# Re-pacing attention beside the feed-forward: denser head pairs in down stages, exps ahead of squares, an earlier third batch, two up tiles held back

## The chip, the cores and the metric

The kernel runs on one core of one Trainium2 chip. The metric is the device time of one execution in microseconds (us). The core has five engines that run side by side: TensorE (PE in the profile, with its weight loads as PEld), VectorE (DVE), ScalarE (ACT), GpSimd (POOL) and SyncE (SP, which here only issues transfers). Each runs its own instructions in the order of the program, and semaphores make one wait for another.

## The reference, cut to what matters

```python
# q: 8 batches x 16 heads x 384 x 64;  k, v: 8 x 4 x 384 x 64   (four q heads share one k/v head)
scores = 1/sqrt(64) * q @ k^T                # per head 384 x 384
attn   = exp(scores - max) / sum
x      = attn @ v                            # 3072 tokens x 1024
h      = max(x @ w_in, 0)                    # "up":   1024 -> 2048
out    = (h*h) @ w_out                       # "down": 2048 -> 1024, float32
```

## The kernel before

A generator yields the feed-forward of one batch after another in small pieces of TensorE work; a main loop walks over the head pairs (two heads at once, 8 pairs per batch) and, between the steps of a pair, takes as many pieces as a credit allows ("filler"). So ScalarE can compute exps while TensorE does feed-forward. A batch's attention output must be transposed by a DMA into `xT` before its feed-forward may begin.

TensorE works in two halves of 64 rows that run at the same time (in the traces a matmul of 64 rows and 384 columns lasts 323 ns, and a pair of them enters each 162 ns). `push` writes the pieces for the low half at once and puts those for the high half into a queue; two clocks of the program's own (`clock["lo"]`, `clock["hi"]`) decide where the high pieces are merged in. These clocks are a plan made while the program is built; nothing measures them on the chip.

```python
def catch_up(until):                       # merges the queued high-half pieces
    while behind:
        job = behind[0]
        begin = max(clock["hi"], job["ready"])
        if begin > until:
            return
        ns, fn = job["hi"].pop(0)
        ...
        if not job["hi"]:
            behind.pop(0)
            ...
            if job["done"]:
                job["done"]()
...
def row_scores(p, half):                   # half a head pair: three score matmuls, then one exp
    ...
    both([piece(i) for i in range(3)])     # always into the same three PSUM banks, sc 0..2
    R.add("scalar", lambda e: e.activation(expT[p % NEX][:, 3 * half:3 * half + 3, :], sc_ps[:, 0:3, 0:S], AF.Exp, scale=0.125), ...)
...
def row_up(b, c, r, then=None):            # one up tile: 16 half-row matmuls
    ...
    def done():
        R.add("vector", lambda e: e.tensor_scalar_max(hr[r][:, :], acc[:, 0:S], 0.0), ...)             # relu
        R.add("scalar", lambda e: e.activation(h2T[b % 2][:, c, :], hr[r][:, :], AF.Square), ...)
        if then:
            then()
...
LULL = 11000.0
PER_PAIR = {1: 2600.0, 2: 3650.0, 3: 3650.0, **{b: 4800.0 for b in range(4, B + 1)}}    # filler, ns per pair
...
for n in range(NPB, NP + 1):
    b, c = n // NPB, n % NPB
    per = PER_PAIR[b]
    ahead = (per - 600.0) / 2
    ...
    if n == 2 * NPB:                       # the lull: no head pairs for 11 us
        fill(ahead)
        row_attend(n - 1)
        fill(2600.0)
        prepare(2)                         # transposes of k and q of batch 2, by DMA
        prepare_v(2)
        fill(LULL - 2600.0)
        ready[0] = 1
    if n < NP:
        row_scores(n, 0)
    fill(ahead)
    if n > NPB and n != 2 * NPB:
        row_attend(n - 1, ...)
    if n < NP:
        row_scores(n, 1)
    if 2 * NPB < n < (B - 1) * NPB:
        ...                                # prepare(b + 1) at c == 4, prepare_v(b + 1) at c == 7
    fill(per - ahead)
    ready[0] = max(0, b - 1)               # which batch's feed-forward may start
```

The down stages of batches 2 to 7 work on pairs of batches and on sums of blocks (seven products instead of eight, as in Strassen's method). Those sums (`a_late`, on DVE) need the squares of the last up tiles, so the end of the up stage of a pair of batches is a chain: up tile, relu, square, sums, next product.

The softmax here doesn't subtract the row's maximum and nothing guards it: scores larger than these inputs give would overflow.

## Time and profile before

| | before |
|---|---|
| time, median | 435.67 us (435.36 to 437.12) |
| PE busy, PEld busy | 95%, 67% |
| granted TensorE clock | 1.0 |
| chain of waits | PE 85%, DVE 6%, ACT 6% |

From the page of the kernel before: busy times, the rows of TensorE and its clock in 40 slices, the chain that ended last, and the groups of exps and squares (count, then busy us and mean ns of one, then idle us before them and its releaser).

```profile
PE 410.9 (95%) x6061; PEld 292.2 (67%) x6061; DVE 203.1 (47%) x419; ACT 217.8 (50%) x284; POOL 48.4 (11%) x62
PE   8999888998999998999999998998999999998995
PEclk9999999999999999999999999999999999999999
PE 85%; DVE 6%; ACT 6%; DMA 2%; issue 1%; DVEq 0%
L474 ACT ACTIVATE expT<-sc_ps 128x1152 bf16<-128x1152 f32 x112 | 126.3, 1127 | 85.8 <-PE sc_ps L470 62.7
L529 ACT ACTIVATE h2T<-hr 128x384 bf16<-128x384 f32 x122 | 63.5, 521 | 68.4 <-DVE hr L527 66.8
```

PE is the bound, but 95% overstates how full it is: with only one of the two row halves at work it counts as busy. The Trainium skill ("Perfetto Trace Analysis", section "Identifying the Most-Contended Engine") says that matmul busy time misjudges the distance to the limit and names weight-load busy time (beside the share of peak work) instead. This trace agrees for the whole: PEld is busy 67%, and by stage it goes up and down where PE hardly does. From the windows of the kernel before (start:end, length, then busy us and count per engine, granted clock, DMA share and GB/s):

```profile
36.00:76.00 40.00, 34.66 (x570) 24.05 (x570) 11.92 (x26) 22.73 (x27) 4.22 (x4) 1.00 1.12 162
146.00:176.00 30.00, 27.22 (x490) 21.86 (x486) 15.22 (x31) 19.37 (x27) 0.83 (x1) 1.00 0.61 105
256.00:306.00 50.00, 46.60 (x772) 37.03 (x769) 23.21 (x50) 30.57 (x43) 4.96 (x5) 1.00 0.54 65
366.00:396.00 30.00, 27.81 (x321) 16.00 (x319) 13.46 (x27) 10.46 (x20) 0.00 (x0) 1.00 0.02 4
```

Between 36 and 76 us PE is busy for 34.66 of 40 us and PEld for 24.05: here the prediction's count of matmuls finds the most lost, 9.8 us. The waits view (engine, line and tile that waited, whom it waited for: us in total, times, longest) says on what:

```profile
ACT h2T L529 <- DVE hr L527: 66.8, 80, 2.2
PE sc_ps L470 <- ACT expT L474: 6.0, 11, 0.7
PE f_ps L638 <- DVE a_late L580: 3.1, 3, 1.3
PE f_ps L521 <- DMA xT<-o_sb: 1.9, 2, 1.3
PE sc_ps L521 <- DMA xT<-o_sb: 1.7, 1, 1.7
```

And the timeline of one head pair in that stage (start, length, engine, line, tiles; in brackets the idle time before and who ended it):

```profile
46.88 0.56 DVE L527 TENSOR_SCALAR hr<-f_ps 128x384 f32<-128x384 f32 x1 [0.65 <-PE po L484]
47.48 0.52 ACT L529 ACTIVATE h2T<-hr 128x384 bf16<-128x384 f32 x1 [1.31 <-DVE hr L527]
47.91 1.11 ACT L474 ACTIVATE expT<-sc_ps 128x1152 bf16<-128x1152 f32 x1
...
49.07 0.50 PE L470 MATMUL sc_ps<-qT,kT 64*128 64x384 bf16 x3 [0.58 <-ACT expT L474]
```

The scores for the exp at 47.91 were issued at 46.81, but ACT first waits for the relu, does the square, and only then the exp; the next scores, which need the same PSUM banks, start at 49.07 after an idle PE.

### The profile page before, as it was taken

What the parts mean: (1) busy time and instruction counts of PE and PEld (TensorE: products, weight loads), DVE (VectorE), ACT (ScalarE), POOL (GpSimd) and SP (SyncE); (2) the same over time, 40 slices, a digit from 0 to 9 for tenths busy, and PEclk for the clock granted to TensorE, in tenths of its full rate; (3) what the DMA queues carried; (4) which work ended last, traced back from release to release, by engine and by line L of the source; (5) the groups of instructions that cost most, each with busy time, mean ns of one, the idle gap of its engine ahead of it and who ended that gap; (6) DMA issues with size and microseconds to landing.
All of it is one profiled execution on the core that took longest, in us unless ns stands there. A gap on an engine that the chain in (4) does not pass through costs nothing.

```text
span 433.3 us, 13205 instructions
## 1 busy us (share of the span) xinstructions
PE 410.9 (95%) x6061; PEld 292.2 (67%) x6061; DVE 203.1 (47%) x419; ACT 217.8 (50%) x284; POOL 48.4 (11%) x62
## 2 busy tenths in 40 slices
PE   8999888998999998999999998998999999998995
PEld 4665665686877777886666787876766787554552
DVE  2664332276522554465564344454654445455442
ACT  4865663066654666565443576665444464332010
POOL 5831010003002100210003000220000000000000
PEclk9999999999999999999999999999999999999999
DMA  8999995739913981195228930296223210000222
GB/s 231 196 197 204 205 183 68 161 108 105 154 52 78 190 138 25 24 129 116 93 70 143 199 98 20 31 129 110 73 74 98 92 44 22 2 2 0 98 98 97
DMA packets 96103, 45.02 MB, mean 104 GB/s; under 512 B 74416, under 2 KB 90032, under 8 KB 96048
## 3 DMA queue, kind: packets, MB, share of 16 engines
q0 software_dynamic: 34288, 16.65, 31.3%
q1 hardware_dynamic: 58720, 25.28, 26.4%
q10 hardware_dynamic: 3040, 2.26, 1.7%
q8 instruction: 47, 0.77, 0.8%
q14 instruction: 8, 0.07, 0.1%
HBM read 35.65 MB, written 12.58 MB: 111 GB/s over the span
## 4 chain that ended last, share of the span: by engine, by line
PE 85%; DVE 6%; ACT 6%; DMA 2%; issue 1%; DVEq 0%
PE f_ps L521 15%; PE sc_ps L521 13%; PE sc_ps L638 12%; PE f_ps L638 11%; PE po L484 11%; PE sc_ps L470 7%; PE sc_ps L562 5%; ACT expT L474 4%; PE f_ps L562 4%; DVE hr L527 2%; ACT h2T L529 2%; DMA xT<-o_sb 2%; PE f_ps L764 2%; PE f_ps L278 1%; PE sc_ps L361 1%; DVE a_late L580 1%
## 5 line engine op out<-in xcount | busy, mean ns | idle before, releaser
L474 ACT ACTIVATE expT<-sc_ps 128x1152 bf16<-128x1152 f32 x112 | 126.3, 1127 | 85.8 <-PE sc_ps L470 62.7
L521 PE MATMUL sc_ps<-xT,w_in_sb 64*128 64x384 bf16 x992 | 151.4, 323 | 1.7 <-DMA xT<-o_sb 1.7
L521 PE MATMUL f_ps<-xT,w_in_sb 64*128 64x384 bf16 x960 | 144.4, 323 | 2.2 <-DMA xT<-o_sb 1.9
L529 ACT ACTIVATE h2T<-hr 128x384 bf16<-128x384 f32 x122 | 63.5, 521 | 68.4 <-DVE hr L527 66.8
L521 PEld LDWEIGHTS sc_ps<-xT,w_in_sb 64*128 64x128 f16 x992 | 83.8, 94 | 15.6 <-DMA xT<-o_sb 2.1
L521 PEld LDWEIGHTS f_ps<-xT,w_in_sb 64*128 64x128 f16 x960 | 80.1, 94 | 18.6 <-DMA xT<-o_sb 2.6
L484 PEld LDWEIGHTS po<-v_aug,expT 64*128 64x128 bf16 x2016 | 76.6, 94 | 17.2 <-DVE o_sb L494 7.6
L484 PE MATMUL po<-v_aug,expT 64*128 64x65 bf16 x2016 | 81.5, 190 | 2.7 <-DVE o_sb L494 2.7
L470 PE MATMUL sc_ps<-qT,kT 64*128 64x384 bf16 x336 | 57.0, 323 | 6.3 <-ACT expT L474 6.0
L527 DVE TENSOR_SCALAR hr<-sc_ps 128x384 f32<-128x384 f32 x62 | 34.6, 557 | 47.1 <-PE sc_ps L521 34.5
L527 DVE TENSOR_SCALAR hr<-f_ps 128x384 f32<-128x384 f32 x60 | 33.3, 557 | 39.9 <-PE f_ps L521 22.6
L638 PE MATMUL sc_ps<-w_out_sb,a_late 64*128 64x512 f16 x176 | 41.9, 376 | 0.0
L562 PE MATMUL sc_ps<-w_out_sb,h2T 64*128 64x512 f16 x192 | 40.2, 376 | 0.0
L562 PE MATMUL f_ps<-w_out_sb,h2T 64*128 64x512 f16 x192 | 40.0, 376 | 0.0
L638 PE MATMUL f_ps<-w_out_sb,h2T 64*128 64x512 f16 x160 | 38.7, 376 | 0.0
L638 PE MATMUL f_ps<-w_late,h2T 64*128 64x512 f16 x160 | 38.4, 376 | 0.0
L470 PEld LDWEIGHTS sc_ps<-qT,kT 64*128 64x128 bf16 x336 | 23.5, 94 | 16.7 <-ACT expT L474 13.0
L494 DVE TENSOR_TENSOR o_sb<-po,rinv 128x384 bf16<-128x384 f32 x56 | 31.2, 557 | 1.9
L492 DVE RECIPROCAL rinv<-po 128x6 f32<-128x6 f32 x56 | 11.0, 196 | 43.9 <-PE f_ps L562 18.9
L638 PE MATMUL sc_ps<-w_late,h2T 64*128 64x512 f16 x128 | 31.0, 376 | 0.0
L638 PE MATMUL sc_ps<-w_out_sb,h2T 64*128 64x512 f16 x128 | 30.9, 376 | 0.0
L580 DVE TENSOR_TENSOR y_sb<-sc_ps,y_sb 128x512 f32<-128x512 f32 x20 | 13.7, 691 | 29.6 <-PE sc_ps L638 20.8
(101 smaller groups left out, 420.7 us busy)
## 6 DMA issues: line engine op xcount, KB each, us to landing
out_dram<-y_sb SPq DMA_DIRECT2D x47, 256.0 KB, 2.2
q_next<-in_q_dram POOLq DMA_DIRECT2D x7, 768.0 KB, 10.7
w_in_sb<-in_moe_w_in_dram POOLq DMA_DIRECT2D x8, 512.0 KB, 12.3
w_out_sb<-in_moe_w_out_dram POOLq DMA_DIRECT2D x2, 2048.0 KB, 33.4
k_st<-in_k_dram POOLq DMA_DIRECT2D x7, 192.0 KB, 3.6
v_st<-in_v_dram POOLq DMA_DIRECT2D x7, 192.0 KB, 11.9
xT<-o_sb SPq DMA_TRANSPOSE x56, 2.5
w_late<-in_q_dram ACTq DMA_DIRECT2D x1, 768.0 KB, 8.7
```

Of the source, the lines that this page charges most:

```text
L470: "tensor", lambda pe: pe.matmul(sc_ps[:, i, 0:S], kt[rows, j * 128:(j + 1) * 128], qt[rows, :]),
L474: R.add("scalar", lambda e: e.activation(expT[p % NEX][:, 3 * half:3 * half + 3, :], sc_ps[:, 0:3, 0:S], AF.Exp, scale=0.125), reads=[("sc ...
L484: "tensor", lambda pe: pe.matmul(po_v[:, f % NJ, f // NJ, :], expT[p % NEX][rows, 2 * j + f % 2, f // 2 * 128:f // 2 * 128 + 128], v_aug[b ...
L492: R.add("vector", lambda e: e.reciprocal(rinv_v, po_v[:, :, :, D:D + 1]), reads=["po"], writes=[("rinv", p % 2)])
L494: R.add("vector", lambda e: e.tensor_tensor(o_sb[p % NO][:, :, :, :], po_v[:, :, :, 0:D], rinv_v.to_broadcast([128, NJ, 2, D]), ALU.mult), ...
L521: "tensor", lambda pe: pe.matmul(acc[:, 0:S], w_in_sb[rows, kc, c * 128:(c + 1) * 128], xT[b % NXT][rows, kc, :], start=(h == 0 and kc == ...
L527: R.add("vector", lambda e: e.tensor_scalar_max(hr[r][:, :], acc[:, 0:S], 0.0), reads=[key], writes=[("hr", r)])
L529: R.add("scalar", lambda e: e.activation(h2T[b % 2][:, c, :], hr[r][:, :], AF.Square), reads=[("hr", r)], writes=h2(b, c))
L562: "tensor", lambda pe: pe.matmul(acc, h2T[b % 2][rows, c, i * 128:(i + 1) * 128], w_out_sb[rows, c, jj * 512:(jj + 1) * 512], start=(h == ...
L580: R.add("vector", lambda e: e.tensor_tensor(out_ap, a, b, op), reads=reads, writes=writes)
L638: "tensor", lambda pe: pe.matmul(acc, lhs[rows], right[rows, c], start=(first and h == 0 and c == 0), stop=(h == 1 and c == NHC - 1), skip ...
L764: m = pe.matmul(acc[:, 0:S], w_in_sb[:, kc, c * 128:(c + 1) * 128], xT[b % NXT][:, kc, :], start=(kc == 0), stop=(kc == NKC - 1))
```

## The change

Its intent: (1) exps overtake squares in ACT's order, by putting each square into the program 750 ns of the planned clock after its tile; (2) the filler per head pair depends on the kind of stage, less beside down stages (3.8 us from batch 4 on) than beside up stages (5.8 us), so pairs stand closer in down stages; batch 1 gets 3.2 us instead of 2.6; (3) batch 2 is prepared during batch 1 and the lull shrinks; (4) the last two up tiles of the first batch of a pair are held back to the end of the pair's up stage, as cover for the sums; (5) a batch's feed-forward starts 3.5 us of the planned clock after its last x was sent; (6) in the last batch GpSimd squares every second tile.

```diff
+    late = []
+
+    def settle(until=float("inf")):
+        while late and late[0][0] <= until:
+            late.pop(0)[1]()
+
     def catch_up(until):
@@
             begin = max(clock["hi"], job["ready"])
+            settle(min(begin, until))
@@
+            turned[b] = turned.get(b, 0) + 1
+            if turned[b] == NPB:
+                usable[b] = clock["hi"] + 3500.0
@@ row_up
-            R.add("scalar", lambda e: e.activation(h2T[b % 2][:, c, :], hr[r][:, :], AF.Square),
-                  reads=[("hr", r)], writes=h2(b, c))
-            if then:
-                then()
+            def square():
+                if b == B - 1 and c % 2:
+                    R.add("gpsimd", lambda e: e.tensor_tensor(h2T[b % 2][:, c, :], hr[r][:, :], hr[r][:, :], ALU.mult), ...)
+                else:
+                    R.add("scalar", lambda e: e.activation(h2T[b % 2][:, c, :], hr[r][:, :], AF.Square), ...)
+                if then:
+                    then()
+
+            late.append((clock["hi"] + 750.0, square))
@@ feed_forward
+    HELD = 2
-        order = list(range(first, NFC))
-        if paired and b % 2:
-            order = [c for g in range(NHC) for c in (g, g + NHC)]
+        order = [(b, c) for c in range(first, NFC)]
+        if paired:
+            order = [(b, c) for g in range(NHC) for c in (g, g + NHC)] + [(b - 1, c) for c in range(NFC - HELD, NFC)] \
+                if b % 2 else order[:-HELD]
@@ all_feed_forward
-            while ready[0] < b:
+            while usable.get(b, float("inf")) > clock["lo"]:
@@
-    LULL = 11000.0
-    PER_PAIR = {1: 2600.0, 2: 3650.0, 3: 3650.0, **{b: 4800.0 for b in range(4, B + 1)}}
+    PACE = {1: (3200.0, 3200.0), 2: (3700.0, 3100.0), 3: (3700.0, 3100.0), **{b: (5800.0, 3800.0) for b in range(4, B + 1)}}
@@ main loop (fill now takes a share of a pair)
-            fill(2600.0)
-            prepare(2)
-            prepare_v(2)
-            fill(LULL - 2600.0)
-            ready[0] = 1
+            fill(1.2)
@@
-        if 2 * NPB < n < (B - 1) * NPB:
-            if c == 4:
+        if NPB < n < (B - 1) * NPB:
+            if c == (4 if b > 1 else 6):
                 prepare(b + 1)
```

(A pair's filler is now split in fixed shares of 0.4 and 0.6 around the two score halves; before, the first share was 0.38 to 0.44.)

More of the change, by code (lines that the diff above doesn't have):

```diff
@@ L424, in catch_up @@
                     job["done"]()
+        settle(until)
     def push(lo, hi, done=None, prev=None, frees=()):
@@ L476, in row_scores @@
               reads=[("sc", i) for i in range(3)], writes=[("expT", p % NEX, 3 * half + i) for i in range(3)])
+    last_av = [None]
+    turned, usable, upped = {}, {0: 0.0}, set()
     def row_attend(p, then=None):
@@ L496, in done @@
                   reads=["po", ("rinv", p % 2)], writes=[("o_sb", p % NO, x) for x in range(2)])
+            assert b - NXT in upped or b < NXT
             landed = put_x(p)
+            turned[b] = turned.get(b, 0) + 1
+            if turned[b] == NPB:
+                usable[b] = clock["hi"] + 3500.0
             if then:
@@ L501, in row_attend @@
         lo, hi = ([piece(r, f, j) for f in range(2 * NJ) for j in range(NJ)] for r in range(2))
-        push(lo, hi, done)
+        last_av[0] = push(lo, hi, done, last_av[0])[0]
     def h2(b, c, i=None):
@@ L528, in done @@
                   reads=[key], writes=[("hr", r)])
-            R.add("scalar", lambda e: e.activation(h2T[b % 2][:, c, :], hr[r][:, :], AF.Square),
-                  reads=[("hr", r)], writes=h2(b, c))
-            if then:
-                then()
+            def square():
+                if b == B - 1 and c % 2:
+                    R.add("gpsimd", lambda e: e.tensor_tensor(h2T[b % 2][:, c, :], hr[r][:, :], hr[r][:, :], ALU.mult),
+                          reads=[("hr", r)], writes=h2(b, c))
+                else:
+                    R.add("scalar", lambda e: e.activation(h2T[b % 2][:, c, :], hr[r][:, :], AF.Square),
+                          reads=[("hr", r)], writes=h2(b, c))
+                if then:
+                    then()
+            late.append((clock["hi"] + 750.0, square))
         lo, hi = ([piece(h, kc) for kc in range(NKC)] for h in range(2))
@@ L536, in row_up @@
         last_up[0] = job
-        return total
+        return "up", total
     ys = [0]
@@ L575, in row_down @@
                 jobs[i], total = push(lo, hi, done if end else None, jobs[i], (banks[i],) if end else ())
-                yield total
+                yield "down", total
     def tensor_op(out_ap, a, b, op, reads, writes):
@@ L675, in p1 @@
             q["p1"], t = product(1, m, q["i"], (0, 0, 0), q["e"], True, done)
-            return t
+            return "down", t
         def rest(q):
@@ L683, in run @@
             def run(n, bank, first, done, prev=None, frees=()):
-                return product(n, m, i, sl, bank, first, done, prev, frees)
+                job, t = product(n, m, i, sl, bank, first, done, prev, frees)
+                return job, ("down", t)
             bank = next_bank()
@@ L736, in part @@
                     return f0, f1, fn
-                return product(3, m, i, q["slots"], None, True, [part(0, 384), part(384, 512)])[1]
-            return product(3, m, i, q["slots"], q["g"], False, c12, q["p5"], (q["g"],))[1]
+                return "down", product(3, m, i, q["slots"], None, True, [part(0, 384), part(384, 512)])[1]
+            return "down", product(3, m, i, q["slots"], q["g"], False, c12, q["p5"], (q["g"],))[1]
         q = dict(i=0)
@@ L743, in down_pair @@
         until(last_up[0])
+        settle()
+        upped.update((b0, b1))
         for i in range(NJ):
@@ L774, in up_step @@
                   reads=[("hr", r)], writes=h2(b, c))
-        return (k1 - k0) * 165
+        return "up", (k1 - k0) * 165
     def feed_forward(b):
@@ L783, in feed_forward, with half @@
         paired = b >= 2
-        order = list(range(first, NFC))
-        if paired and b % 2:
-            order = [c for g in range(NHC) for c in (g, g + NHC)]
-        slots = {}
-        def half(x):
-            slots.setdefault(0, None) or slots.update({0: take_sums()})
-            a_sums(0, slots[0], (1, 2, 3, 4), x * NHC // 2, (x + 1) * NHC // 2)
-        for n, c in enumerate(order):
+        order = [(b, c) for c in range(first, NFC)]
+        if paired:
+            order = [(b, c) for g in range(NHC) for c in (g, g + NHC)] + [(b - 1, c) for c in range(NFC - HELD, NFC)] \
+                if b % 2 else order[:-HELD]
+        slots = {}
+        def half(x, which):
+            if 0 not in slots:
+                slots[0] = take_sums()
+            a_sums(0, slots[0], which, x * NHC // 2, (x + 1) * NHC // 2)
+        then = {}
+        if paired and b % 2:
+            then = {NHC - 1: lambda: half(0, (1, 2, 3, 4)), NFC - 1: lambda: half(1, (1, 2, 3)), len(order) - 1: lambda: half(1, (4,))}
+        for n, (bb, c) in enumerate(order):
             if by_rows[0]:
-                pairs = paired and b % 2
-                yield row_up(b, c, tiles[0] % NHR, (lambda: half(0)) if pairs and n == NHC - 1 else
-                             (lambda: half(1)) if pairs and n == NFC - 1 else None)
+                yield row_up(bb, c, tiles[0] % NHR, then.get(n))
             else:
                 for k in range(0, NKC, 4):
-                    yield up_step(b, c, k, k + 4, tiles[0] % 2, tiles[0] % NHR)
+                    yield up_step(bb, c, k, k + 4, tiles[0] % 2, tiles[0] % NHR)
             tiles[0] += 1
@@ L810, in feed_forward @@
         elif not paired:
+            last = last_up[0]
             for jj in range(2):
-                yield from row_down(b, jj)
-    ready = [0]
+                for kind in row_down(b, jj):
+                    yield kind
+                    if last and last["over"]:
+                        upped.add(b)
     def all_feed_forward():
         for b in range(B):
-            while ready[0] < b:
+            while usable.get(b, float("inf")) > clock["lo"]:
                 if carry:
@@ L824, in all_feed_forward, with fill @@
         while carry:
-            yield carry.pop()() or 1.0
+            yield carry.pop()()
     ffn = all_feed_forward()
     credit = [0.0]
-    LULL = 11000.0
-    PER_PAIR = {1: 2600.0, 2: 3650.0, 3: 3650.0, **{b: 4800.0 for b in range(4, B + 1)}}
-    def fill(ns):
-        credit[0] += ns
+    PACE = {1: (3200.0, 3200.0), 2: (3700.0, 3100.0), 3: (3700.0, 3100.0), **{b: (5800.0, 3800.0) for b in range(4, B + 1)}}
+    pace = {"up": 1.0, "down": 1.0}
+    def fill(share):
+        credit[0] += share
         while credit[0] > 0:
-            t = next(ffn, 0)
-            if not t:
+            kind = next(ffn, 0)
+            if not kind:
                 credit[0] = 0.0
                 return
-            credit[0] -= t
+            credit[0] -= kind[1] / pace[kind[0]]
     turns = [lambda banks=RING, g=g: first_kT(g, 1, banks) for g in range(HKV)]
@@ L893, in bass_gqa_attention__then__ffn_squared_relu_kernel @@
     by_rows[0] = True
+    credit[0] = 0.0
     for n in range(NPB, NP + 1):
         b, c = n // NPB, n % NPB
-        per = PER_PAIR[b]
-        ahead = (per - 600.0) / 2
+        pace["up"], pace["down"] = PACE[b]
         def load_next(landed):
@@ L903, in bass_gqa_attention__then__ffn_squared_relu_kernel @@
         if n == 2 * NPB:
-            fill(ahead)
+            fill(0.4)
             row_attend(n - 1)
-            fill(2600.0)
-            prepare(2)
-            prepare_v(2)
-            fill(LULL - 2600.0)
-            ready[0] = 1
+            fill(1.2)
         if n < NP:
             row_scores(n, 0)
-        fill(ahead)
+        fill(0.4)
         if n > NPB and n != 2 * NPB:
@@ L922, in bass_gqa_attention__then__ffn_squared_relu_kernel @@
                 prepare_v(b + 1)
-        fill(per - ahead)
-        ready[0] = max(0, b - 1)
-    ready[0] = B
-    while next(ffn, None):
-        pass
+        fill(0.6)
+    while (kind := next(ffn, 0)) != 0:
+        if kind is None:
+            clock["lo"] += 100.0
+            catch_up(clock["lo"])
     R.add("sync", lambda e: e.nop(), reads=[("out", b, i, jj, c) for b in range(B) for i in range(NJ) for jj in range(2) for c in (0, 384)])
```

## The prediction

> **What bounds it now.** TensorE. The page gives PE 95% busy, granted clock 1.0; the chain of waits is 85% PE, 6% DVE, 6% ACT. The Trainium skill ("Perfetto Trace Analysis", section "Identifying the Most-Contended Engine") warns that matmul busy time misjudges headroom and names weight-load busy instead; the trace agrees: weight loads are 67% busy, and the array's two 64-row halves run side by side (a 64x384 matmul lasts 323 ns, but a pair enters each 162 ns). So I counted matmuls per 10 us window and costed them by issue distance (162 ns for 384 columns, 216 for 512, 33 for 65, two halves at once). From 26 us on, about 27 of 400 us are lost. Estimated by stage: 36-76 us 9.8; 96-116 2.4; 146-176 3.5; pair ends near 200, 300, 390 about 1.0, 1.6, 1.8; around 268 2.0; the rest small.
>
> **Causes, from the timeline and the waits.** In 40-66 us one head pair takes 4.87 us although its PE work is 3.67: ACT runs in order, an exp stands behind a square that waits for its relu (ACT waits 66.8 us for relus in all), and scores wait for exps (6.0 us of full PE idle, more half-idle). Three waits for transposed x (171, 268, 366 us; 3.6 us idle). At pair ends PE waits for relu, square and 0.44 us sums (3.1 us idle, more half-idle).
>
> **What the change does.** No TensorE work goes. Squares enter ACT's order 750 ns of the program's own clock after the tile, so exps pass them. Batch 1 gets 3.2 us of feed-forward per head pair instead of 2.6; the attention-free lull (11 us of filler) goes, since batch 2 is prepared during batch 1. A batch's feed-forward starts 3.5 us after its last x was sent: no late x. Two up tiles (2.6 us) cover the sums at pair ends. In the last batch GpSimd squares every second tile: nothing gained.
>
> Expected: 36-85 us loses 5 instead of 9.8; 96-116 loses 1.3 (0.68 us weight sums still delay relus); 146-176 and 256-306 lose 1 to 1.5 each instead of 3.5 and 4.5; pair ends 0.3 each; tail wait gone. Gains about 14 us.
>
> **What it costs.** From the order of instructions, about five head-pair halves now have only 0.9 us of PE work between two groups of scores, where exp and scores need 1.72 us (38.42 to 40.14 us): about 0.75 us each, 3.7 us. Batch 2's keys land at 63.3 us, its queries at 68.5 (DMA landings); their transposes sit ahead of three x transposes in the sync queue, so batch 2's first scores (about 74 us) and batch 1's first up tile (79 us) are nearly late: 1 us.
>
> Net gain about 10 us: **425.5 us**, range 419 to 431. Faster by over 2% (below 427) 0.62, within 2% 0.36, slower 0.02. The end with feed-forward alone grows from 66 to about 78 us of PE work, harmless at full rate.
>
> **What would show it.** Head pairs of batch 1 near 4.4 us apart; ACT's wait for relus well below 66.8 us; PE idle for transposed x 1 us or less; PE's waits for sums under 1 us; gaps of 0.5 to 0.9 us before scores in down stages after 150 us; no stretch without exps near 80 us.
>
> **What would make it wrong.** Relus over 750 ns late behind other DVE work, so that exps still wait; batch 2's transposes late by several us; the single attention accumulator limiting denser pairs; GpSimd squares slow enough to hold relu buffers. Upward: short halves cost less than I think, then 420.

## The result, and the profile after

| | before | after |
|---|---|---|
| time, median | 435.67 us | 425.35 us (424.85 to 425.75) |
| ratio, 95% interval | | 0.9756 (0.9732 to 0.9780): faster by over 2% |
| PE busy, PEld busy | 95%, 67% | 97%, 74% |
| granted clock | 1.0 | 0.997 to 1.0 |

A ratio is the mean time of one kernel's fast runs over that of the kernel before's of the same rounds, so it is not quite the ratio of the medians. The lines of the page after:

```profile
PE 409.2 (97%) x6061; PEld 311.7 (74%) x6061; DVE 202.5 (48%) x419; ACT 213.0 (50%) x276; POOL 55.1 (13%) x70
PE   7999999999999999999999999999999999999995
PE 89%; ACT 4%; DVE 4%; DMA 2%; issue 1%; ACTq 0%; POOL 0%; DVEq 0%
```

The work is the same (PE 409 against 411 us, 6061 matmuls); the chain of waits has more PE and less of the others. The windows of the same stages after:

```profile
36.00:76.00 40.00, 38.63 (x630) 29.79 (x630) 13.48 (x28) 22.84 (x27) 4.20 (x4) 1.00 1.28 194
146.00:176.00 30.00, 29.48 (x497) 23.18 (x492) 16.58 (x33) 19.49 (x28) 4.12 (x4) 1.00 0.42 74
256.00:306.00 50.00, 49.56 (x806) 39.16 (x802) 26.79 (x55) 30.66 (x43) 4.96 (x5) 1.00 0.53 77
366.00:396.00 30.00, 29.30 (x316) 22.18 (x313) 14.96 (x30) 5.30 (x10) 4.96 (x6) 1.00 0.08 28
```

From 36 to 76 us TensorE is now busy 38.63 instead of 34.66 us and does 630 matmuls instead of 570. Counting matmuls and costing them by their issue distance, as the prediction did, the work lost from 26 us to the end falls from about 27 to about 17 us (an estimate: full windows of 10 us count about 10.37 us of work, because matmuls at both edges are counted, and that is taken off). The waits:

```profile
ACT h2T L550 <- DVE hr L542: 52.6, 55, 5.0
PE sc_ps L478 <- ACT expT L482: 2.6, 5, 0.6
PE po L495 <- DVE o_sb L505: 2.1, 7, 0.4
```

TensorE's waits for transposed x and for the sums are gone from the list. In the first stage ACT now has this order:

```profile
47.69 0.56 DVE L542 TENSOR_SCALAR hr<-sc_ps 128x384 f32<-128x384 f32 x1 [0.65 <-PE po L495]
48.13 1.13 ACT L482 ACTIVATE expT<-sc_ps 128x1152 bf16<-128x1152 f32 x1 [1.06 <-PE sc_ps L478]
49.16 0.52 ACT L550 ACTIVATE h2T<-hr 128x384 bf16<-128x384 f32 x1
```

The exp (48.13) starts right after its scores, although the relu is still running; the square comes after it.

What is left of "scores wait for exps" has another look. In a down stage, where ACT has nothing but exps:

```profile
219.72 0.49 PE L478 MATMUL sc_ps<-qT,kT 64*128 64x384 bf16 x3
220.28 1.13 ACT L482 ACTIVATE expT<-sc_ps 128x1152 bf16<-128x1152 f32 x1 [1.47 <-PE po L495]
221.46 0.49 PE L478 MATMUL sc_ps<-qT,kT 64*128 64x384 bf16 x3 [0.61 <-ACT expT L482]
```

Scores and exp of one half need 1.74 us (219.72 to 221.46), and between these two groups of scores the program has only 3 down matmuls and 18 of attention; with the scores themselves that is about 0.9 us of TensorE work. These are the "short halves" of the prediction.

### The profile page after: what moved, and what is told of

It reads as the page before. It is cut to its first block, busy times and chain, and to the rows that moved or that the text cites. A ratio compares the mean times of both kernels' runs of the same rounds, so it can differ in the third digit from the quotient of the medians.

```text
span 422.8 us, 13245 instructions
## 1 busy us (share of the span) xinstructions
PE 409.2 (97%) x6061; PEld 311.7 (74%) x6061; DVE 202.5 (48%) x419; ACT 213.0 (50%) x276; POOL 55.1 (13%) x70
## 4 chain that ended last, share of the span: by engine, by line
PE 89%; ACT 4%; DVE 4%; DMA 2%; issue 1%; ACTq 0%; POOL 0%; DVEq 0%
PE sc_ps L536 16%; PE f_ps L536 16%; PE sc_ps L661 12%; PE f_ps L661 12%; PE po L495 12%; PE sc_ps L478 8%; PE f_ps L585 5%; ACT expT L482 3%; PE sc_ps L585 3%; PE f_ps L791 2%; DMA w_late<-in_q_dram 1%; DVE o_sb L505 1%; PE po L378 1%; PE sc_ps L361 1%; PE sc_ps L300 1%
## 5 line engine op out<-in xcount | busy, mean ns | idle before, releaser
L536 PE MATMUL sc_ps<-xT,w_in_sb 64*128 64x384 bf16 x992 | 146.6, 322 | 0.7 <-DVE hr L542 0.7
L536 PE MATMUL f_ps<-xT,w_in_sb 64*128 64x384 bf16 x960 | 142.2, 323 | 0.0
L550 ACT ACTIVATE h2T<-hr 128x384 bf16<-128x384 f32 x114 | 58.3, 519 | 52.6 <-DVE hr L542 52.6
L585 PE MATMUL sc_ps<-w_out_sb,h2T 64*128 64x512 f16 x192 | 41.5, 376 | 0.0
L661 PE MATMUL sc_ps<-w_out_sb,h2T 64*128 64x512 f16 x128 | 30.9, 376 | 0.0
```

The lines of the kernel that those rows point to most:

```text
L536: "tensor", lambda pe: pe.matmul(acc[:, 0:S], w_in_sb[rows, kc, c * 128:(c + 1) * 128], xT[b % NXT][rows, kc, :], start=(h == 0 and kc == ...
L585: "tensor", lambda pe: pe.matmul(acc, h2T[b % 2][rows, c, i * 128:(i + 1) * 128], w_out_sb[rows, c, jj * 512:(jj + 1) * 512], start=(h == ...
L661: "tensor", lambda pe: pe.matmul(acc, lhs[rows], right[rows, c], start=(first and h == 0 and c == 0), stop=(h == 1 and c == NHC - 1), skip ...
```

## The experiments

Each is timed in five rounds against the kernel before on the same chip; its medians there were 435.45 to 435.89 us. Names starting with a are the changed kernel with parts undone, b is the kernel before with one part added, c and g are the changed kernel with another pace.

| run | what it is | median us | ratio to before |
|---|---|---|---|
| (after) | the change | 425.35 | 0.9756 |
| a_no_late | squares at once | 427.86 | 0.9821 |
| b_late | before, late squares only | 432.15 | 0.9921 |
| a_no_hold | no held tiles | 430.97 | 0.9897 |
| a_even_pace | old even filler | 422.43 | 0.9701 |
| c_late4_even | old filler in batches 4 to 7 | 421.84 | 0.9671 |
| c_flat | pace without short or naked halves (naked: no filler at all) | 421.89 | 0.9675 |
| g_even_halves | denser still | 431.01 | 0.9893 |
| c_best | more filler in batch 1 | 432.27 | 0.9931 |
| a_act_sq | no squares on GpSimd | 424.61 | 0.9756 |
| a_lull, a_lull2 | third batch late again | 433.41 (wrong result), 429.76 | 0.9957, 0.9854 |

### Late squares: a_no_late and b_late

```diff
-            late.append((clock["hi"] + 750.0, square))
+            square()
```

> The changed kernel with one part undone: each square enters ScalarE's order right after its relu, not 750 ns later. TensorE's order is the same. Theory (exps stuck behind squares were the largest loss): about 4 us slower than the changed kernel, near 429.5 us, the loss in 36-76 us, where exps wait for relus again (pairs of batch 1 above 4.6 us apart). Rival (the thicker filler of 3.2 us per pair removed that loss by itself): within 1 us of 425.4.

Measured: 427.86 us, 2.5 us slower than the change. Both theories missed: less than the 4 us of the first, more than the 1 us of the rival. ACT's wait for relus is back, and TensorE's wait for exps doubles (it was 2.6 us in the change):

```profile
ACT h2T L550 <- DVE hr L542: 80.3, 73, 5.0
PE sc_ps L478 <- ACT expT L482: 5.3, 10, 0.7
```

Pairs of batch 1 are 4.81 us apart again (36.32 to 65.15 us), but by the count of matmuls only about 1 us of the loss lies between 36 and 76 us, where all of it was expected (estimate).

b_late does the opposite: `late`, `settle` and the late `square` are put into the kernel before, and nothing else.

> The kernel before with one part added: squares enter ScalarE's order 750 ns later, nothing else; TensorE's order stays that of before. Theory: 4 to 6 us faster than before, 430 to 431.5 us, most of it between 36 and 76 us. Rival (pace): under 2 us faster, above 433.5 us.

Measured: 432.15 us, 3.3 us faster than before (435.45), again between the two. TensorE's wait for exps nearly goes (it was 6.0 us), but a second line shows why it is not more:

```profile
PE sc_ps L478 <- ACT expT L482: 0.9, 2, 0.5
PE f_ps L649 <- DVE a_late L591: 4.3, 3, 1.8
```

TensorE's wait for the sums at the ends of the up stages rises from 3.1 to 4.3 us: the square is later, so the sums are. What the exps gain is partly given back there. The order of ACT is worth 2.5 to 3.3 us, and part of the thicker filler's effect is the same loss seen from the other side.

### Held tiles: a_no_hold

```diff
-    HELD = 2
+    HELD = 0          # and the slices and sums adapted: order[:NFC - HELD], half(1, (1, 2, 3, 4)) at the 16th tile
```

> The changed kernel with no up tiles held to a pair's end. Theory: the three pair ends lose 1.0, 1.5 and 1.5 us again: 428 to 429.5 us, and TensorE's wait for the sums is 2 to 3 us again. Rival (the late squares alone already cover the sums): within 1 us of 425.4.

Measured: 430.97 us, 5.6 us slower than the change, more than expected. TensorE waits for the sums:

```profile
PE f_ps L661 <- DVE a_late L603: 4.4, 3, 1.9
```

That is 4.4 us of full idle at three ends (longest 1.9 us, at 295 us, where DVE itself waited 1.54 us for a square); the rest of the 5.6 us is half-idle time around it (estimate, by difference; the count of matmuls puts about 1.7, 2.1 and 2.2 us of loss at the three ends and almost none elsewhere). The late squares lengthen what the held tiles cover (3.1 us of waits before, 4.3 in b_late), so the cover is probably worth more inside the change than in the kernel before; no run adds it there.

### The pace: a_even_pace and c_late4_even

```diff
-    PACE = {1: (3200.0, 3200.0), 2: (3700.0, 3100.0), 3: (3700.0, 3100.0), **{b: (5800.0, 3800.0) ...}}
+    PACE = {1: (2600.0, 2600.0), 2: (3650.0, 3650.0), 3: (3650.0, 3650.0), **{b: (4800.0, 4800.0) ...}}
```

> The changed kernel with the old even filler per head pair (2.6, 3.65, 4.8 us, the same beside up and down stages); everything else of the change stays. Theory: the pace itself gains little, because what it saves early it pays in short halves: 425 to 428 us, no gaps of 0.5 us or more before scores in down stages after 150 us. Rival (the pace is the main gain): 430 us or more.

Measured: 422.43 us, 2.9 us *faster* than the whole change, and below the 425 to 428 us expected. So the pace, the first thing in the change's description, costs time. By the order of instructions the sum of what the short halves lack (1.72 us minus the TensorE work from one group of scores to the next, scores included, where that is positive) is 7.4 us in the changed kernel from its first row-paired scores on and 4.7 us in this one, a difference of 2.7 us (estimate).

The next run undoes the pace in batches 4 to 7 only, `(4800.0, 4800.0)` there. It takes away the four late short halves, but also thins the filler beside the up stages of these batches:

> The changed kernel with the old even filler (4.8 us per pair) in batches 4 to 7 only; batches 1 to 3 keep the new pace. By the order of instructions this removes just the four late halves with 0.86 to 0.97 us of TensorE work (3.3 us of stalls, estimated), and leaves the one near 126 us. Theory (those short halves are the cost of the dense pace): 422 to 422.8 us. Rival (the even-paced kernel won its 3 us in batches 1 to 3, or by chance of the clock): 424.5 us or slower.

Measured: 421.84 us, 3.5 us faster than the change, where 2.6 to 3.4 us had been expected. The line of TensorE waiting for exps:

```profile
PE sc_ps L478 <- ACT expT L482: 0.5, 1, 0.5
```

It was 2.6 us in 5 waits. The four waits that left are the late short halves: about 3.5 us of time, 2.1 us of it visible as full idle. That the gain is theirs, and not that of the up stages, the count of matmuls shows: the four 10 us windows that hold them (from 186, 216, 296 and 326 us) lose about 3.1 us in the change and nothing in this run, and the others from 146 to 336 us about 1.4 and 1.3 us (estimate). Only one of the five short halves lies before batch 4; the new pace of batches 1 to 3 gains about 1 us (0.6 us between the medians 422.43 and 421.84; 1.3 us by the ratios).

### A pace chosen by counting: c_flat

```diff
+    PACE = {1: (3000.0, 3000.0), 2: (3400.0, 3400.0), 3: (3400.0, 3400.0), **{b: (5200.0, 4600.0) ...}}
```

> Everything of the change, with the pace chosen by the order of instructions alone so that neither short halves (none below 1.2 us of TensorE work after 36 us but the first) nor halves without any filler occur: 3.0 us in batch 1, 3.4 in 2 and 3, 5.2 beside up and 4.6 beside down stages after that. Theory (short and naked halves are what the pace decides): 420.5 to 422 us, granted clock 0.997 or more. Rival (other waits, such as stores or transposed x, take over): above 422.5 us.

Measured: 421.89 us, as expected, and the same as c_late4_even. Both beat the kernel before by 3.3% and the change by 3.5 us.

### Denser, or fuller: g_even_halves and c_best, and what the clock does

g_even_halves was to remove the short halves by giving each half exactly one product (3.45 us per pair, split evenly, in down stages from batch 4 on).

> The changed kernel, with the filler beside down stages of batches 4 to 7 cut from 3.8 to 3.45 us per pair and split evenly, so that exactly one product (1.73 us) stands in each half; the pairs are even denser there. The four halves with only 0.86 us of work after 190 us are gone, by the order of instructions; two short halves at 0.86 us and less remain before that. Theory (short halves are the cost of the dense pace): 2 to 3 us faster than the changed kernel, 422.5 to 423.5 us. Rival (density itself costs, through the single attention accumulator or ScalarE): 425 us or slower.

Measured: 431.01 us, 5.7 us slower than the change: the theory's number is far off, though the four late short halves did go. The chain of waits of this run shows one long break (start, length, what):

```profile
236.43 0.57 DVE o_sb L505
236.99 0.14 SPq L396
237.13 0.04 issue
237.18 2.84 DMA out_dram<-y_sb
240.05 0.04 issue
240.09 0.58 ACT y_sb L718
240.67 1.04 ACT expT L482
```

A copy on ACT waited for an output buffer, which waited for its store; the store stood in the sync queue behind an x transpose, which held the queue until 236.99 us, when its own `o_sb` was ready. (The two q transposes of the next batch had held the queue before, 4.49 us from 230.64, but were through at 235.13.) The exp stood behind the copy on ACT, and TensorE stood still for 3.9 us. No run tried this pace with another order in the sync queue, so what the density alone costs stays open. Then, in the windows of the same run:

```profile
238.00:240.00 2.00, 0.00 (x0) 0.00 (x0) 0.43 (x1) 0.00 (x0) 0.00 (x0) 1.00 0.70 198
241.00:242.00 1.00, 0.24 (x2) 0.13 (x4) 0.00 (x0) 0.71 (x1) 0.00 (x0) 0.50 0.46 178
242.00:247.00 5.00, 5.00 (x45) 3.41 (x43) 0.69 (x1) 1.13 (x1) 0.00 (x0) 0.50 0.29 94
248.00:252.00 4.00, 4.00 (x65) 3.25 (x62) 1.25 (x2) 1.65 (x3) 0.00 (x0) 1.00 0.13 29
```

The granted clock halves for about 7 us. The Trainium skill ("TensorE: Matmul & The Clock Gate", Part 1) says that the clock drops to half after an idle window of about 3.4 us; here TensorE stood still from 237.86 us, and the clock dropped about 3 us later (0.91 is the mean of the window from 240 to 241 us, so about 240.8 us), in agreement with the page. It came back after 6.83 us. All four executions ran at a mean clock of 0.991 to 0.995, so this belongs to the kernel.

c_best keeps the old pace after batch 1 and gives batch 1 3.7 us per pair.

> Everything of the change except the dense pace: 3.7 us of filler per pair in batch 1, the old even 3.65 and 4.8 us after it. By the order of instructions no half after 90 us has less than 1.4 us of work. Theory: like the even-paced kernel (422.4 us), with 1.5 to 3 us less lost between 36 and 76 us: 419.5 to 421 us, the fastest of all. Rival (batch 1's loss comes from DMA landings or the accumulator, not from too little filler): 422 us or more.

Measured: 432.27 us, 12 us slower than the theory's middle. I had counted wrongly: my count of short halves took several halves with nothing at all between their scores as one. With more filler in batch 1, the first feed-forward is used up before the second batch's x has come, and at 80 us halves stand without filler. From the windows:

```profile
80.00:81.00 1.00, 0.14 (x2) 0.00 (x0) 0.64 (x2) 0.82 (x1) 0.00 (x0) 1.00 0.44 172
82.00:83.00 1.00, 0.00 (x0) 0.00 (x0) 0.00 (x0) 1.00 (x1) 0.00 (x0) 0.99 0.38 83
92.00:96.00 4.00, 4.00 (x48) 2.92 (x47) 0.78 (x3) 1.13 (x1) 1.64 (x2) 0.50 0.22 32
96.00:99.00 3.00, 3.00 (x22) 2.09 (x19) 0.57 (x1) 0.04 (x1) 1.78 (x3) 0.50 0.89 90
```

No single gap before it was longer than 1.2 us, yet the clock went to half at 83 us and stayed there until 100 us, though TensorE was busy without a break from 92 us on. All six executions had a mean clock of 0.979 to 0.982. So running out of filler for a few halves costs far more than the gaps themselves. c_flat was chosen with the count mended.

### Squares on GpSimd: a_act_sq

```diff
-                if b == B - 1 and c % 2:
+                if False:
```

> The changed kernel with all squares of the last batch on ScalarE again, none on GpSimd. TensorE's order is the same. Theory (GpSimd squares bring nothing, ScalarE is idle there): within 0.7 us of 425.4. Rival (they relieve ScalarE): 1 us slower or more; or they are slow and hold the sums back: 0.7 us faster or more, with DVE no longer waiting for GpSimd before the sums.

Measured: 424.61 us (424.38 to 426.62), ratio 0.9756, the same as the change. A square takes 0.83 us on GpSimd and 0.52 us on ACT. The Trainium skill ("GPSIMD Engine Reference", section 3.1) gives about 2.6 cycles per element for a two-input operation; an estimate from that, 384 elements at the 1.2 GHz that the page states, is 0.83 us, and the trace agrees. In the last batch ACT has room (5.3 of 30 us busy from 366 to 396 us in the change), so where the square is done does not matter.

### The third batch, and the rule for starting: a_lull and a_lull2

These start from a_even_pace, put `prepare(2)` back behind batch 1 into an 11 us lull, and use the old rule (`ready[0]`).

> The even-paced kernel (422.4 us) with the third batch prepared late again, after batch 1, in an 11 us stretch without head pairs, and the old rule for when a feed-forward may start. Theory (early preparation puts attention ahead of the feed-forward, so no x comes late): TensorE's waits for transposed x return, 3 to 4 us, so 425.5 to 427 us. Rival (the lull is full-rate work and costs nothing): within 1 us of 422.4.

The result was wrong (relative error 0.03). A check of each read while the program was built showed three matmuls of batch 3's first up tile put into the program before the transpose of the last x chunk that they read: the old rule counted loop turns and did not look whether the transpose had been issued. Its time is therefore not used. Its waits can be read with that reserve, and late x is back in them, as expected:

```profile
PE sc_ps L536 <- DMA xT<-o_sb: 4.3, 3, 2.8
```

The mended run, whose result is right, also waits until that transpose is in the program:

```diff
-            while ready[0] < b:
+            while ready[0] < b or (b and turned.get(b, 0) < NPB):
```

> The run with the late third batch, mended: a feed-forward now also waits until the last transpose of its batch has been put into the program, so the result is right. Otherwise the even-paced kernel (422.4 us) with the third batch prepared after batch 1 in an 11 us lull; one half is left without filler. Theory: x waits of TensorE return, 2 to 4 us, and one naked half adds about 2 us with no clock loss: 425.5 to 428 us. Rival (the lull costs nothing): within 1.5 us of 422.4.

Measured: 429.76 us, 7.3 us slower than a_even_pace and beyond both theories. TensorE's waits for x did not return (0.3 us). Instead the feed-forward came to its end and was held back, so that a half ran naked; between 156 and 176 us the count of work shows about 5 us lost (estimate). Times were spread (426.99 to 431.74 us) with mean clocks of 0.988 to 0.997. The profiled execution is the fastest of them, and its clock was full until the last few us: the 4.5 us that it is slower than a_even_pace's (426.99 against 422.45 us) are not the clock. That the lull, with the rule that it needs, is not free is shown; whether the clock makes up the rest is not.

One part could be judged without a chip. The changed kernel with the old rule `ready[0]` in place of `usable` gives the same order of instructions on all engines as with it, and so does the even-paced kernel. So the 3.5 us rule changes nothing in either program.

## Why the prediction was right or wrong

The time was right: 425.35 us against 425.5, within the range, and faster by over 2% as given the better chance. Point by point:

- **ACT's order in the first stage: right in kind.** The exp passes the square, ACT's wait for relus fell from 66.8 to 52.6 us, and undoing it makes it 80.3 us. The stage from 36 to 86 us was to lose 5 us; the count gives about 4.5. Pairs of batch 1 start 4.65 us apart (six pairs from 36.10 to 63.99 us), a little more than the 4.4 predicted. Alone, the reordering is worth 2.5 to 3.3 us.
- **Short halves: right, and nearly to size.** Five were predicted at 3.7 us together; taking away four of them gained 3.5 us. The full idle is four gaps of 0.37 to 0.61 us, at and below the lower end of the 0.5 to 0.9 predicted. (The fifth wait in the list, 0.5 us at 38.40 us, stood in the kernel before too; the fifth short half, at 127 us, left 0.06 us.)
- **Sums at the pair ends: right in kind, too small.** TensorE's wait for them is gone. I had put the gain at about 3.5 us (4.4 lost, 0.9 left); undoing the held tiles costs 5.6. The missed term is at least in part the interaction: late squares make the wait longer (3.1 to 4.3 us in b_late), and the held tiles must cover that too.
- **"A batch's feed-forward starts 3.5 us after its last x was sent: no late x": wrong step, right outcome.** The x waits are gone, but the rule is not why; without it the program is the same. What remains is that attention runs further ahead, because it is no longer held up for the lull. a_lull points that way: with the lull back, TensorE waits 4.3 us for x. But its result was wrong, and in a_lull2 the rule that it needs turned late x into missing filler, so this cause is likely, not shown.
- **"The attention-free lull goes": only half.** ACT's wait for scores there fell from 14.23 to 7.15 us; `fill(1.2)` is still there. I had said there would be no stretch without exps near 80 us; there is one from 72 to 79 us.
- **Batch 2's transposes nearly late, 1 us: not seen.** Its first scores came at 78.76 us without a wait, and no wait for x shows. That 1 us of cost was not there.
- **GpSimd squares gain nothing: right** (0.9756 both ways).

That the sum came out within 0.2 us is luck: errors of both signs met, as the pair ends gained about 2 us more than given, and the reordering less. And the part that names the change, the denser pace beside down stages, costs about 3 us (2.9 and 3.5 in two runs); the gain comes from the held tiles, the order of ACT and, as far as a_lull2 shows it, the early preparation.

## What to carry to other kernels

Where a loop alternates small steps on two engines, find the shortest time that one round of the slower engine needs (here 1.72 us for scores and exp) and count, in the order of instructions, that no round holds less work of the other engine than that; an average filler is not enough. Two changes to one chain are not independent: moving squares back is paid at the next place that waits for them, and needs its cover there. And fullness has a cliff: when filler runs out for a few rounds, TensorE's clock can halve, and the loss is several times the gap (in c_best two gaps of 1.2 us, then 17 us at half clock).

## What the Trainium skill lacked or had wrong

- "TensorE: Matmul & The Clock Gate", section "HAM oscillation": its rule is to have no TensorE gaps above about 3.4 us. That is too weak. In c_best no gap was longer than 1.2 us, but TensorE was busy for only 0.64 of the 3 us from 80 to 83 us, and the clock halved; in a_lull one gap of 2.8 us did it. The page's next section says that frequent short idles can do this, but gives no measure of how little work is too little.
- The same page, Part 1: the full clock is to return after about 3.4 us of sustained work, counted in windows of 3.41 us that run freely. The lengths agree: the half clock lasted 3.41 us in a_lull, 6.83 in g_even_halves and 17.07 in c_best (from the clock records), which is one, two and five windows. But in c_best TensorE was busy without a break in the last two of the five, and only the second brought the clock back. So a window without a break is not enough; the page has no threshold. By the count of matmuls (estimate), the windows that brought it back held 0.44 to 0.55 of the work of a full-rate window, those that did not 0.40 or less.
